# Scores and V·dO of a decode attention backward: eight short matmuls per chunk replaced by two of 512 columns and a selection

## Chip, cores, metric

One core of a Trainium2 chip. The metric is the time of one execution in microseconds (us) of device time; several executions per kernel, medians given.

## The reference

One decode step (one query row, 32 heads, 8192 cached keys of 128 bf16 each), attention plus a gated MLP in parallel, and the gradients of all inputs but B_x. What matters for the time is the K and V cache and their gradients:

```python
q = xn @ wq                      # 32 heads of 128
s = (q . k_cache) * 128**-0.5    # 8192 scores per head
p = softmax(s);  o = p . v_cache # then @ wo
# backward of one head, dO = grad_out @ wo^T:
dp = v_cache . dO                # 8192 values, "V*dO"
u  = p * (dp - sum(p * dp))
dq = u . k_cache;  dK = u x q;  dV = p x dO     # outer products, 2 MB each
```

Per head 4 MB are read (K, V) and 4 MB written (dK, dV).

## The kernel before

A head's K (or V) lies in SBUF as 128 partitions x 64 keys x 128 dimensions. The sums over the dimensions need the dimensions on the partitions, so TensorE transposes. To halve that work, pairs of bf16 are transposed as one fp32 word: `T` makes four 128x128 fp32 transposes (a "chunk", 8 of the 64 keys of every partition) into PSUM, and ScalarE copies them to SBUF. `M` then reads the words as bf16 again; every second value is of one parity.

```python
def T(h, kind, c):
    W3 = kv_tiles[(kind, h)][:].bitcast(F32).rearrange("p (i w) -> p i w", w=P)
    pT = pst()                                  # one of 4 PSUM buffers
    for k in range(4):
        nc.tensor.transpose(pT[:, k * P:(k + 1) * P], W3[:, 4 * c + k, :], ident_f[:])
    KT = kt_tile()
    nc.scalar.copy(KT[:]..., pT[:])

def M(h, kind, c):                              # chunk: stationary; q (or dO) pair: moving
    ...
    for k in range(4):
        i = 4 * c + k
        for par in range(2):
            o = ZW + J * (2 * par + a) - 2 * i  # 64-column window, zero but for columns 2i, 2i+1
            nc.tensor.matmul(S_[kind][:, 0:J], lhsT=KTb[:, k, par, :], rhs=S_["cz"][:, o:o + J],
                             start=(i == 0 and par == 0), stop=(par == 1), ...)
```

The result is one [128, 64] block of scores, keys on the partitions as in the cache. After it come the softmax (`mx`, `mx_bc`, `expo`, `zsum`), the o sum and the dq sum (64 matmuls each, K or V as stationary side), and VectorE's outer products, which overwrite K and V in place; the tile is then stored. Loads and stores go through one FIFO of ten 2 MB slots (`fifo` on SyncE): a load needs a slot whose store is done. TensorE alternates T and M: T(c), M(c-2), T(c+1), M(c-1), and so on, over the 8 K chunks and the 8 V chunks of a head. Before head 2 the MLP runs.

## Time and profile before

| | before |
|---|---|
| time, median | 749.19 us (748.56 to 749.82, 4 runs) |
| bytes moved | 304.63 MB |
| one head, from 255 to 691 us | 21.8 us |
| one head while TensorE had work in stock, 106 to 233 us | 18.1 us |

A head is counted from the first matmul of its o sum to that of the next head's, starts read from the timeline.

The page of the kernel before (span; busy time of TensorE's matmuls and weight loads and of the others; granted clock, DMA share and GB/s in 40 slices; the queue that brings instructions; the chain that ended last, by engine; groups of instructions with busy time, mean ns of one, and idle time before them):

```profile
span 745.6 us, 25013 instructions
...
PE 596.1 (80%) x11263; PEld 568.4 (76%) x11263; DVE 447.8 (60%) x739; ACT 333.4 (45%) x668; POOL 30.4 (4%) x45
...
PEclk9997799999999889999999999998999899988965
DMA  8999999999999999999999999999999999999991
GB/s 327 387 413 421 426 425 425 395 427 426 416 426 427 428 421 428 425 428 425 424 424 429 426 425 417 415 417 424 420 413 425 418 417 419 419 415 418 408 402 72
...
q8 instruction: 88, 1.44, 0.7%
...
DMA 48%; PE 39%; DVE 8%; issue 2%; ACT 1%; SPq 0%; ACTq 0%; DVEq 0%
...
L274 PE MATMUL pT<-ident_f,kv 128*128 128x128 f32 x2048 | 337.1, 289 | 67.4 <-DMA kv<-in_A_k_cache_dram 62.4
...
L293 PEld LDWEIGHTS <-KT 128*128 128x128 bf16 x4096 | 196.8, 100 | 17.7 <-issue 10.6
...
L293 PE MATMUL dA<-cz,KT 128*128 128x64 bf16 x2048 | 107.6, 197 | 8.0 <-ACT qd L310 5.8
```

About half of the chain is DMA, and GB/s stays near 424. The groups mislead in one point: a matmul of L293 is given 197 ns, and there are 4096, so they seem to cost hundreds of us. But these are latencies of pipelined instructions. What one costs is the distance between starts. The timeline of TensorE (start us, us, what) shows it, two transposed chunks (L274) and two M (L293):

```profile
185.77 0.40 PE L293 MATMUL sA<-cz,KT 128*128 128x64 bf16 x8
186.01 0.63 PE L274 MATMUL pT<-ident_f,kv 128*128 128x128 f32 x4
186.48 0.40 PE L293 MATMUL sA<-cz,KT 128*128 128x64 bf16 x8
186.71 0.63 PE L274 MATMUL pT<-ident_f,kv 128*128 128x128 f32 x4
```

From one M to the next M are 186.48 - 185.77 = 0.71 us. Of that the eight matmuls of M take 186.01 - 185.77 = 0.24 us, 30 ns each, weight load included; the four transposes take 0.47.

TensorE's own waits (engine, what waits, for what: us in total, times, longest):

```profile
PE pT L274 <- DMA kv<-in_A_k_cache_dram: 62.4, 22, 5.4
PE hb L358 <- DVE U L365: 14.3, 32, 0.4
```

It waits for K loads, so data come later than TensorE needs them. The waits of the queue that issues loads and stores:

```profile
SPq L101 <- DMA out_dram<-kv: 543.6, 57, 16.9
SPq L101 <- DVE kv L379: 31.9, 11, 7.2
```

A load waits for an earlier store to free its slot: the queue is held by the DMA, not by compute. Windows of 100 us in the middle (us, busy time and count of each engine, granted clock, DMA share, GB/s):

```profile
core 0: us, PE busy (x) PEld busy (x) DVE busy (x) ACT busy (x) POOL busy (x), PEclk, DMA share, GB/s
300.00:400.00 100.00, 80.38 (x1565) 77.11 (x1564) 59.59 (x87) 46.02 (x92) 3.26 (x4) 0.97 1.01 426
400.00:500.00 100.00, 79.86 (x1488) 76.89 (x1485) 56.76 (x93) 45.94 (x93) 3.26 (x4) 0.93 1.01 421
```

### The profile page before, as it was taken

What the parts mean: (1) busy time and instruction counts of PE and PEld (TensorE: products, weight loads), DVE (VectorE), ACT (ScalarE), POOL (GpSimd) and SP (SyncE); (2) the same over time, 40 slices, a digit from 0 to 9 for tenths busy, and PEclk for the clock granted to TensorE, in tenths of its full rate; (3) what the DMA queues carried; (4) which work ended last, traced back from release to release, by engine and by line L of the source; (5) the groups of instructions that cost most, each with busy time, mean ns of one, the idle gap of its engine ahead of it and who ended that gap; (6) DMA issues with size and microseconds to landing.
All of it is one profiled execution on the core that took longest, in us unless ns stands there. A gap on an engine that the chain in (4) does not pass through costs nothing.

```text
span 745.6 us, 25013 instructions
## 1 busy us (share of the span) xinstructions
PE 596.1 (80%) x11263; PEld 568.4 (76%) x11263; DVE 447.8 (60%) x739; ACT 333.4 (45%) x668; POOL 30.4 (4%) x45
## 2 busy tenths in 40 slices
PE   1987698999999779888787897778798788979920
PEld 1886598988998778877686896778798787869820
DVE  4169937677767456656555763646556664656580
ACT  1641055555565355535355553445454353554500
POOL 0100200000000100001000000000000000000000
PEclk9997799999999889999999999998999899988965
DMA  8999999999999999999999999999999999999991
GB/s 327 387 413 421 426 425 425 395 427 426 416 426 427 428 421 428 425 428 425 424 424 429 426 425 417 415 417 424 420 413 425 418 417 419 419 415 418 408 402 72
DMA packets 29136, 304.63 MB, mean 409 GB/s; under 512 B 2836, under 2 KB 5972, under 8 KB 12644
## 3 DMA queue, kind: packets, MB, share of 16 engines
q1 hardware_dynamic: 22736, 276.39, 88.5%
q0 software_dynamic: 5984, 26.30, 8.8%
q8 instruction: 88, 1.44, 0.7%
q10 hardware_dynamic: 308, 0.33, 0.1%
q14 instruction: 20, 0.16, 0.1%
HBM read 151.67 MB, written 151.34 MB: 406 GB/s over the span
## 4 chain that ended last, share of the span: by engine, by line
DMA 48%; PE 39%; DVE 8%; issue 2%; ACT 1%; SPq 0%; ACTq 0%; DVEq 0%
DMA kv<-in_A_k_cache_dram 31%; PE pT L274 17%; DMA out_dram<-kv 13%; PE hb L358 6%; PE hb L373 4%; PE sA L293 4%; DMA kv<-in_A_v_cache_dram 4%; PE dA L293 4%; DVE kv L379 3%; DVE U L365 1%; PE sA L320 1%; PE dh_ps L462 1%; PE hb L363 1%; PE acc L536 1%; PE gu_ps L451 1%
## 5 line engine op out<-in xcount | busy, mean ns | idle before, releaser
L274 PE MATMUL pT<-ident_f,kv 128*128 128x128 f32 x2048 | 337.1, 289 | 67.4 <-DMA kv<-in_A_k_cache_dram 62.4
L276 ACT COPY KT<-pT 128x512 f32<-128x512 f32 x512 | 299.3, 586 | 182.6 <-PE pT L274 149.4
L274 PEld LDWEIGHTS pT<-ident_f,kv 128*128 128x128 f32 x2048 | 224.6, 145 | 71.5 <-issue 69.6
L293 PEld LDWEIGHTS <-KT 128*128 128x128 bf16 x4096 | 196.8, 100 | 17.7 <-issue 10.6
L379 DVE TENSOR_TENSOR kv<-qd,U 128x4096 bf16<-128x4096 bf16 x64 | 146.0, 2284 | 0.0
L379 DVE TENSOR_TENSOR kv<-qd,P 128x4096 bf16<-128x4096 bf16 x64 | 143.4, 2282 | 0.0
L293 PE MATMUL dA<-cz,KT 128*128 128x64 bf16 x2048 | 107.6, 197 | 8.0 <-ACT qd L310 5.8
L293 PE MATMUL sA<-cz,KT 128*128 128x64 bf16 x2048 | 102.7, 192 | 0.4 <-issue 0.3
L358 PEld LDWEIGHTS <-kv 128*128 128x128 bf16 x2048 | 81.7, 106 | 16.5 <-issue 16.5
L358 PE MATMUL hb<-P,kv 128*128 128x64 bf16 x2048 | 82.3, 202 | 14.3 <-DVE U L365 14.3
L375 ACT COPY od_g<-hb 128x2 f32<-128x2 f32 x32 | 5.1, 160 | 160.9 <-PE hb L373 160.9
L373 PE MATMUL hb<-U,kv 128*128 128x64 bf16 x2048 | 70.8, 194 | 5.1 <-issue 5.1
L373 PEld LDWEIGHTS <-kv 128*128 128x128 bf16 x2048 | 66.9, 98 | 6.0 <-issue 5.8
L349 DVE SCALAR_TENSOR_TENSOR U<-dA,P 128x64 bf16<-128x64 f32 x32 | 7.4, 232 | 93.7 <-PE dA L293 93.7
L316 DVE TENSOR_REDUCE mrow<-sA 128x1 f32<-128x64 f32 x32 | 7.2, 224 | 79.5 <-PE sA L293 79.5
L365 DVE SCALAR_TENSOR_TENSOR U<-dA,hb,P 128x128 bf16<-128x128 f32 x32 | 11.4, 355 | 36.3 <-PE hb L363 36.3
L429 DVE SCALAR_TENSOR_TENSOR wq_g<-wq_g,side 128x512 bf16<-128x512 bf16 x40 | 27.3, 683 | 0.0
L340 DVE RECIPROCAL rZ<-sA 128x1 f32<-128x1 f32 x32 | 5.4, 168 | 35.9 <-PE sA L334 35.0
L233 DVE SCALAR_TENSOR_TENSOR side<-wo_g,g_bc 128x640 bf16<-128x640 bf16 x32 | 26.2, 818 | 0.3
L323 DVE TENSOR_REDUCE negM<-sA 128x1 f32<-128x128 f32 x32 | 9.3, 291 | 18.6 <-PE sA L320 18.6
L424 POOL DMA_DIRECT2D out_dram<-wo_g x8 | 6.1, 761 | 295.5 <-DVE cz L298 262.3
L433 POOL DMA_DIRECT2D out_dram<-wq_g x8 | 6.9, 863 | 254.3 <-DVE wq_g L431 254.3
(134 smaller groups left out, 311.5 us busy)
## 6 DMA issues: line engine op xcount, KB each, us to landing
out_dram<-kv SPq DMA_DIRECT2D x64, 2048.0 KB, 31.8
kv<-in_A_k_cache_dram SPq DMA_DIRECT2D x32, 2048.0 KB, 26.9
kv<-in_A_v_cache_dram SPq DMA_DIRECT2D x32, 2048.0 KB, 26.9
out_dram<-wo_g POOLq DMA_DIRECT2D x8, 640.0 KB, 12.1
out_dram<-wq_g POOLq DMA_DIRECT2D x8, 640.0 KB, 13.3
wq_g<-in_A_wq_dram POOLq DMA_DIRECT2D x7, 640.0 KB, 13.8
wo_g<-in_A_wo_dram POOLq DMA_DIRECT2D x7, 640.0 KB, 19.5
kv<-in_B_w_dram SPq DMA_DIRECT2D x2, 1728.0 KB, 16.1
```

Source lines behind the costliest of these rows:

```text
L233: nc.vector.scalar_tensor_tensor(junk[:], G_["wo"][:, hh, :], 1.0, g_bc[:], ALU.mult, ALU.mult, accum_out=G_["do"][:, hh:hh + 1])
L274: nc.tensor.transpose(pT[:, k * P:(k + 1) * P], W3[:, 4 * c + k, :], ident_f[:])
L276: nc.scalar.copy(KT[:].rearrange("p k w -> p (k w)"), pT[:])
L293: nc.tensor.matmul(S_[kind][:, 0:J], lhsT=KTb[:, k, par, :], rhs=S_["cz"][:, o:o + J], start=(i == 0 and par == 0), stop=(par == 1), skip_ ...
L320: nc.tensor.matmul(S_["K"][:, J:J + P], lhsT=S_["mrow"][:].to_broadcast([P, P]), rhs=ident_f[:], start=False, stop=True, skip_group_check= ...
L323: nc.vector.tensor_reduce(S_["negM"][:], S_["K"][:, J:J + P], AX.X, ALU.max, negate=True)
L358: nc.tensor.matmul(S_["hb"][:, 0:RW], lhsT=V3[:, j, :], rhs=S_["P2"][:, j, 0:1].to_broadcast([P, RW]), start=(j == 0), stop=(j == J - 1), ...
L363: nc.tensor.matmul(S_["hb"][:, 2 * RW:2 * RW + 1], lhsT=negones_b, rhs=S_["rdot"][:], start=False, stop=True, skip_group_check=True)
L365: nc.vector.scalar_tensor_tensor(S_["U2"][:], S_["V"][:, 0:J].unsqueeze(2).to_broadcast([P, J, 2]), S_["hb"][:, 2 * RW:2 * RW + 1], S_["P2 ...
L373: nc.tensor.matmul(S_["hb"][:, RW:2 * RW], lhsT=K3[:, j, :], rhs=S_["U2"][:, j, 0:1].to_broadcast([P, RW]), start=False, stop=(j == J - 1) ...
L379: nc.vector.tensor_tensor(dst[:, lo * DH:hi * DH].rearrange("p (j a b) -> p j a b", a=DH // 2, b=2), vec.rearrange("p (a b) -> p a b", b=2 ...
L429: nc.vector.scalar_tensor_tensor(wq_g[:, ci, :], wq_g[:, ci, :], 1.0, dqb, ALU.mult, ALU.mult, accum_out=dxa[:, ci, g:g + 1])
```

## The change

The intent is to swap the two operands of M. The transposed chunk becomes the moving operand, all 512 columns at once, and the q (or dO) pair, zero-padded to 128 columns, becomes the stationary one. Eight weight loads and matmuls per chunk become two. The price: the scores come out turned, 16 useful rows of 512 values, so they are copied to SBUF and turned back by four fp32 matmuls with columns of the identity (`selm`), for K and for V.

```diff
-    ps_t = ctx.enter_context(tc.tile_pool(name="ps_t", bufs=4, space=PSUM))
+    ps_t = ctx.enter_context(tc.tile_pool(name="ps_t", bufs=3, space=PSUM))
+    ps_m = ctx.enter_context(tc.tile_pool(name="ps_m", bufs=1, space=PSUM))
 ...
     def M(h, kind, c):
-        for k in range(4):
-            i = 4 * c + k
-            for par in range(2):
-                o = ZW + J * (2 * par + a) - 2 * i
-                nc.tensor.matmul(S_[kind][:, 0:J], lhsT=KTb[:, k, par, :], rhs=S_["cz"][:, o:o + J], ...)
+        for par in range(2):
+            o = QZ0 + P * (2 * a + par) - 2 * c
+            nc.tensor.matmul(S_[kind][:], lhsT=qz[:, o:o + P], rhs=KTb[:, par, :],
+                             start=(c == 0 and par == 0), stop=(c == NCH - 1 and par == 1))
+
+    def ev(h, kind):
+        XS = kt_tile()
+        nc.scalar.copy(XS[:]..., S_.pop(kind)[:])
+
+    def selm(h, kind):
+        for k in range(4):
+            nc.tensor.matmul(S_["m"][:, b0:b0 + J].rearrange("p (c k t) -> p k c t", k=4, t=2)[:, k, :, :],
+                             lhsT=XS[:, k, :], rhs=ident_f[:, 0:2 * NCH].rearrange("p (c t) -> p c t", t=2), ...)
 ...
     def head(h):            # order: K's eviction and selection ahead of the maximum,
         M(h, "K", NCH - 1)
+        ev(h, "K")
+        T(h, "V", 2)
+        fill_qz(h, 1)
+        selm(h, "K")
         mx(h)
-        T(h, "V", 2)
 ...
+        ev(h, "V")          # V's around half of the o sum; a third chunk of the next head ahead of dq
+        o_sum(h, 0, J // 2)
+        selm(h, "V")
         rdot(h)
-        o_sum(h, 0, J // 2)
+        o_sum(h, J // 2, J)
         dsum(h)
-        o_sum(h, J // 2, J)
+        if pre:
+            T(h + 1, "K", 2)
         dq_sum(h)
```

The rest of the diff moves the small reductions to the new PSUM bank `m` and fills the padded operand `qz` in two steps.

More of the change, by code (lines that the diff above doesn't have):

```diff
@@ L258 @@
     hd = {}
-    ZW = J - 2
-    cz_tiles = []
-    for i in range(2):
-        cz = consts.tile([P, ZW + 4 * J], BF16, name=f"cz{i}")
-        nc.vector.memset(cz[:], 0.0)
-        cz_tiles.append(cz)
     NCH = J // 8
+    QZ0 = 2 * (NCH - 1)
+    qz = consts.tile([P, QZ0 + 4 * P], BF16, name="qz")
+    nc.vector.memset(qz[:], 0.0)
     def new_head(h):
-        hd[h] = dict(kt={}, cz=cz_tiles[h % 2])
+        hd[h] = dict(kt={})
     def T(h, kind, c):
@@ L287, in M, with fill_qz @@
         KTb = S_["kt"].pop((kind, c))[:].rearrange("p k w -> p (k w)").bitcast(BF16).rearrange(
-            "p (k t two) -> p k two t", two=2, t=P)
-        for k in range(4):
-            i = 4 * c + k
-            for par in range(2):
-                o = ZW + J * (2 * par + a) - 2 * i
-                nc.tensor.matmul(S_[kind][:, 0:J], lhsT=KTb[:, k, par, :], rhs=S_["cz"][:, o:o + J],
-                                 start=(i == 0 and par == 0), stop=(par == 1), skip_group_check=True)
-    def fill_cz(h):
+            "p (n two) -> p two n", two=2)
+        for par in range(2):
[3 more added lines that the diff above has]
+    def ev(h, kind):
+        S_ = hd[h]
+        XS = kt_tile()
+        nc.scalar.copy(XS[:].rearrange("p k w -> p (k w)"), S_.pop(kind)[:])
+        S_["xs" + kind] = XS
+    def selm(h, kind):
+        S_ = hd[h]
+        if kind == "K":
+            S_["m"] = ps_m.tile([P, 512], F32, name="m", tag="m")
+        b0 = 0 if kind == "K" else J
+        XS = S_.pop("xs" + kind)
+        for k in range(4):
+            nc.tensor.matmul(S_["m"][:, b0:b0 + J].rearrange("p (c k t) -> p k c t", k=4, t=2)[:, k, :, :],
+                             lhsT=XS[:, k, :], rhs=ident_f[:, 0:2 * NCH].rearrange("p (c t) -> p c t", t=2),
+                             start=(kind == "K" and k == 0), stop=True, skip_group_check=True)
+        S_[kind] = S_["m"][:, b0:b0 + J]
+    def fill_qz(h, a):
         g, hh = divmod(h, GH)
-        nc.vector.tensor_copy(hd[h]["cz"][:, ZW:ZW + 4 * J].rearrange("p (k s) -> p k s", s=J)[:, :, 0:2],
-                              grp[g]["cm"][:, :, :, hh, :].rearrange("p t a m -> p (t a) m"))
+        o = QZ0 + 2 * P * a
+        nc.vector.tensor_copy(qz[:, o:o + 2 * P].rearrange("p (t n) -> p t n", n=P)[:, :, 0:2],
+                              grp[g]["cm"][:, :, a, hh, :])
     def rows_pe(h, ps, first):
@@ L319, in mx_bc @@
         S_ = hd[h]
-        nc.tensor.matmul(S_["K"][:, J:J + P], lhsT=S_["mrow"][:].to_broadcast([P, P]), rhs=ident_f[:],
+        nc.tensor.matmul(S_["m"][:, 2 * J:2 * J + P], lhsT=S_["mrow"][:].to_broadcast([P, P]), rhs=ident_f[:],
                          start=False, stop=True, skip_group_check=True)
         S_["negM"] = small.tile([P, 1], F32, name="negM")
-        nc.vector.tensor_reduce(S_["negM"][:], S_["K"][:, J:J + P], AX.X, ALU.max, negate=True)
+        nc.vector.tensor_reduce(S_["negM"][:], S_["m"][:, 2 * J:2 * J + P], AX.X, ALU.max, negate=True)
     def expo(h):
@@ L333, in zsum @@
         S_ = hd[h]
-        nc.tensor.matmul(S_["K"][:, J + P:J + P + 1], lhsT=ones_b, rhs=S_["rsum"][:],
+        nc.tensor.matmul(S_["m"][:, 2 * J + P:2 * J + P + 1], lhsT=ones_b, rhs=S_["rsum"][:],
                          start=False, stop=True, skip_group_check=True)
@@ L339, in probs @@
         rZ = small.tile([P, 1], F32, name="rZ")
-        nc.vector.reciprocal(rZ[:], S_["K"][:, J + P:J + P + 1])
+        nc.vector.reciprocal(rZ[:], S_["m"][:, 2 * J + P:2 * J + P + 1])
         P2 = small.tile([P, J, 2], BF16, name="P2")
@@ L587, in side_v @@
         elif hh == 3 and g + 1 < NG:
-            prep_cm(g + 1, hd[h]["V"][:, 324:324 + 4 * GH])
+            prep_cm(g + 1, hd[h]["m"][:, 324:324 + 4 * GH])
     def side_pe1(h):
@@ L594, in side_pe1 @@
         elif hh == 3 and g + 1 < NG:
-            prep_q(g + 1, hd[h]["V"][:, 320:320 + GH], False)
+            prep_q(g + 1, hd[h]["m"][:, 320:320 + GH], False)
     def side_pe2(h):
@@ L599, in side_pe2 @@
         if hh == 3 and g + 1 < NG:
-            prep_sel(g + 1, hd[h]["V"][:, 324:324 + 4 * GH])
+            prep_sel(g + 1, hd[h]["m"][:, 324:324 + 4 * GH])
     def outers_a(h):
@@ L617, in head @@
         has_prev = h > 0 and h != MLP_AT
-        had = 2 if h != MLP_AT else 0
+        had = (3 if h else 2) if h != MLP_AT else 0
         if nxt:
@@ L623, in head @@
         side_k(h)
+        if had == 3:
+            M(h, "K", 0)
         for c in range(had, NCH):
@@ L631, in head @@
         M(h, "K", NCH - 1)
+        ev(h, "K")
+        T(h, "V", 2)
+        fill_qz(h, 1)
+        selm(h, "K")
         mx(h)
-        T(h, "V", 2)
+        M(h, "V", 0)
+        T(h, "V", 3)
         mx_bc(h)
         side_m(h)
-        M(h, "V", 0)
-        T(h, "V", 3)
-        expo(h)
         M(h, "V", 1)
         T(h, "V", 4)
+        expo(h)
         M(h, "V", 2)
@@ L655, in head @@
         if nxt:
-            fill_cz(h + 1)
-            rows_pe(h + 1, hd[h]["V"][:, 64:64 + 2 * DH], False)
+            fill_qz(h + 1, 0)
+            rows_pe(h + 1, pst()[:, 0:2 * DH], True)
             rows_act(h + 1)
@@ L678 @@
     prep_cm(0, ps_0[:, 8:8 + 4 * GH])
-    fill_cz(0)
+    fill_qz(0, 0)
     rows_pe(0, ps_0[:, 64:64 + 2 * DH], False)
```

## The prediction

> **What bounds the kernel now.** The DMA: the windows of 25 us show a DMA share near 1.0 and about 424 GB/s from 50 to 700 us. From 255 to 691 us a head takes 21.8 us (start of the o sum to the next head's, timeline). TensorE is close behind: from 106 to 233 us, while it had loaded heads in stock, the waits show almost nothing ahead of it and a head took 18.0 us. Later it waits for K loads (62.4 us in all, view of waits). So TensorE has 3.8 us of slack per head.
>
> **What the change does to TensorE, per head.** It removes 256 weight loads and matmuls of 64 columns. They look costly on the page (197 ns each) but are pipelined: their starts are 28.6 ns apart, so a chunk's eight take 0.23 us, and with four transposes a chunk takes 0.70 us. It adds, per chunk, two matmuls of 512 columns. The MLP stage has 256-column bf16 matmuls 108.5 ns apart, weight loads hidden, as the Trainium skill, "TensorE: Matmul & The Clock Gate", section "Back-to-back issue gap", says (N/2.4 + 2.5). So I estimate 215 ns each: 1024 columns streamed in place of 512. The transposes, 110 ns apart, stay; the long matmul hides their first fp32 weight load (now 0.03 us). Chunk 0.87 us against 0.70, 16 chunks: +2.7 us.
> Selection: 8 fp32 matmuls of two passes; beside a short moving side an fp32 weight load holds the next pass about 110 ns (the sum of the exponentials), so twice 0.85 us: +1.7 us.
> Waits: after the last K chunk the eviction (0.59 us) queues behind another on ScalarE, one transpose covers 0.44 us: +0.5. The third transposed chunk ahead of the dq sum shortens the wait for U, the row broadcast no longer waits: -0.4.
> Sum +4.5 us, range 3.3 to 5.5. ScalarE gets two evictions more (1.2 us) and has room.
>
> **On the critical path.** 18.0 + 4.5 = 22.5 us exceeds the DMA's 21.8, so TensorE becomes the bound of the whole run. Before, without DMA waits, the last head's o sum would start at 106 + 29 x 18.0 = 628 us. After: 628 + 32 x 4.5 = 772 us, plus about 25 us for the last head's outer products, gradients and store (without the store backlog of before).
>
> **Predicted: 797 us, range 770 to 824.** Chances: faster by over 2% 0.02, within 2% 0.05, slower by over 2% 0.93.
>
> **What would show it.** TensorE about 95% busy, clock near 1.0 throughout; waits for K loads below 15 us; DMA share about 0.9 in the middle windows; score matmuls 215 ns apart, a chunk 0.87 us; a head 22 to 23 us in every stretch; a selection group 0.8 to 0.9 us; about 0.5 us of wait ahead of K's selection; the SP queue waiting for VectorE more than now.
>
> **What would make it wrong.** The moving operand takes every second bf16, four bytes apart. All wide bf16 moving operands in the trace are contiguous, and the fp32 ones stream at half rate; if the stride halves the rate, a chunk costs 1.3 us and the time is about 1020 us. If selection or waits are smaller than I think, a head falls below 21.8 us, the DMA stays the bound and only the tail of the last three heads grows: about 755 us. Three PSUM buffers instead of four could add waits on ScalarE.

## The result, and the profile after

| | before | after |
|---|---|---|
| time, median | 749.19 us | 787.09 us (786.77 to 787.32, 4 runs) |
| ratio, 95% interval | | 1.0509 (1.0493 to 1.0525) |
| bytes moved | 304.63 MB | 304.30 MB |
| one head | 21.8 us (18.1 with work in stock) | 22.1 us throughout (120 to 739 us) |
| start of the last head's o sum | 707.5 us | 759.3 us |

A ratio here is the mean time of one kernel's runs over that of the other's of the same rounds, so not quite the ratio of the medians quoted.

The page of the changed kernel, the same parts:

```profile
span 785.5 us, 19851 instructions
...
PE 718.0 (91%) x8625; PEld 575.8 (73%) x8703; DVE 449.3 (57%) x770; ACT 365.2 (46%) x732; POOL 30.4 (4%) x45
...
PEclk9998899999999999999999999999999999999995
DMA  8999999999999999999999999999999999995556
GB/s 326 386 410 422 425 421 388 365 347 420 408 407 423 397 415 405 420 396 422 412 408 420 401 415 402 426 392 418 415 400 427 403 415 410 392 366 249 222 216 280
...
q8 instruction: 68, 1.11, 0.5%
...
PE 82%; ACT 8%; DVE 5%; issue 3%; DMA 2%; SPq 0%; ACTq 0%; DVEq 0%
...
L272 PE MATMUL pT<-ident_f,kv 128*128 128x128 f32 x2048 | 310.0, 274 | 5.0 <-DMA kv<-in_A_k_cache_dram 4.9
L289 PE MATMUL sA<-KT,qz 128*128 128x512 bf16 x480 | 151.2, 390 | 2.2 <-issue 0.2
...
L305 PE MATMUL m<-ident_f,KT 128*128 128x16 f32 x512 | 67.4, 264 | 11.1 <-ACT KT L295 11.1
L305 PEld LDWEIGHTS m<-ident_f,KT 128*128 128x128 f32 x512 | 62.1, 191 | 18.7 <-ACT KT L295 18.7
```

The chain that was half DMA is now TensorE for 82%. TensorE's matmuls fill 91% of the span, and its granted clock reads 1.00 in the windows below (mean of the run 0.979). The timeline of TensorE in one head (L272 transposes, L289 long matmuls, L373 o sum, L305 selection of V):

```profile
293.36 0.60 PE L272 MATMUL pT<-ident_f,kv 128*128 128x128 f32 x4
293.80 0.62 PE L289 MATMUL dA<-KT,qz 128*128 128x512 bf16 x2
294.25 0.60 PE L272 MATMUL pT<-ident_f,kv 128*128 128x128 f32 x4
294.69 0.61 PE L289 MATMUL dA<-KT,qz 128*128 128x512 bf16 x2
...
296.58 0.61 PE L289 MATMUL dA<-KT,qz 128*128 128x512 bf16 x2
297.03 1.14 PE L373 MATMUL hb<-P,kv 128*128 128x64 bf16 x32
298.01 1.04 PE L305 MATMUL m<-ident_f,KT 128*128 128x16 f32 x8
298.90 1.14 PE L373 MATMUL hb<-P,kv 128*128 128x64 bf16 x32
```

From one M to the next are 294.69 - 293.80 = 0.89 us, against 0.71. The two long matmuls take 294.25 - 293.80 = 0.45 us, the four transposes 0.44. The selection of V takes 298.90 - 298.01 = 0.89 us. The timeline gives x8 for its four matmuls: an fp32 one runs as two passes. TensorE's waits:

```profile
PE m L305 <- ACT KT L295: 11.1, 32, 0.6
...
PE pT L272 <- DMA kv<-in_A_k_cache_dram: 4.9, 1, 4.9
```

Only one wait for K loads is left, that of the start. The wait ahead of the selection is 0.35 us per head in K's case, in the view's account; from start to start the gap is 0.60 us where an undisturbed one is 0.11, so 0.49. The waits of the queue for loads and stores:

```profile
SPq L102 <- DVE kv L394: 445.8, 47, 12.0
...
SPq L102 <- DMA out_dram<-kv: 44.7, 5, 17.8
```

Before it waited 543.6 us for stores and 31.9 for VectorE's outer products; now 44.7 and 445.8. The outer products come late, it seems because TensorE's results do: the chain, 82% TensorE, fits that. The windows:

```profile
300.00:400.00 100.00, 96.91 (x1156) 77.73 (x1167) 59.62 (x91) 50.61 (x101) 4.91 (x6) 1.00 1.00 410
400.00:500.00 100.00, 96.96 (x1176) 78.16 (x1186) 57.16 (x98) 50.13 (x102) 3.26 (x4) 1.00 1.00 411
```

The DMA share still reads 1.00, although the DMA is no longer what holds the program; only the GB/s have fallen, from about 424 to 410. The Trainium skill, "Perfetto Trace Analysis", section "Identifying the Most-Contended Engine", says that the occupancy of the 16 DMA engines misleads and that the utilization of the memory's bandwidth should be used. This trace agrees.

### The profile page after: what moved, and what is told of

Its sections match the earlier page's. It is cut to its first block, busy times and chain, and to the rows that moved or that the text cites. A ratio compares the mean times of both kernels' runs of the same rounds, so it can differ in the third digit from the quotient of the medians.

```text
span 785.5 us, 19851 instructions
## 1 busy us (share of the span) xinstructions
PE 718.0 (91%) x8625; PEld 575.8 (73%) x8703; DVE 449.3 (57%) x770; ACT 365.2 (46%) x732; POOL 30.4 (4%) x45
## 2 busy tenths in 40 slices
DMA packets 29117, 304.30 MB, mean 387 GB/s; under 512 B 2837, under 2 KB 5973, under 8 KB 12645
## 4 chain that ended last, share of the span: by engine, by line
PE 82%; ACT 8%; DVE 5%; issue 3%; DMA 2%; SPq 0%; ACTq 0%; DVEq 0%
PE pT L272 26%; PE sA L289 13%; PE dA L289 13%; PE hb L373 8%; PE m L305 8%; PE hb L388 8%; ACT KT L274 4%; ACT KT L295 2%; DVE kv L394 2%; DMA kv<-in_A_k_cache_dram 2%; PE m L349 2%; ACT E L344 1%; PE m L335 1%; PE hb L378 1%; PE dh_ps L477 1%
## 5 line engine op out<-in xcount | busy, mean ns | idle before, releaser
L272 PEld LDWEIGHTS pT<-ident_f,kv 128*128 128x128 f32 x2048 | 253.5, 142 | 101.5 <-issue 5.5
L272 PE MATMUL pT<-ident_f,kv 128*128 128x128 f32 x2048 | 310.0, 274 | 5.0 <-DMA kv<-in_A_k_cache_dram 4.9
L289 PE MATMUL sA<-KT,qz 128*128 128x512 bf16 x480 | 151.2, 390 | 2.2 <-issue 0.2
L289 PE MATMUL dA<-KT,qz 128*128 128x512 bf16 x466 | 146.6, 388 | 3.3
L289 PEld LDWEIGHTS <-qz 128*128 128x128 bf16 x1024 | 97.8, 102 | 5.8 <-issue 0.2
L373 PEld LDWEIGHTS <-kv 128*128 128x128 bf16 x2048 | 71.5, 98 | 8.3
L305 PE MATMUL m<-ident_f,KT 128*128 128x16 f32 x512 | 67.4, 264 | 11.1 <-ACT KT L295 11.1
L305 PEld LDWEIGHTS m<-ident_f,KT 128*128 128x128 f32 x512 | 62.1, 191 | 18.7 <-ACT KT L295 18.7
L373 PE MATMUL hb<-P,kv 128*128 128x64 bf16 x2048 | 72.9, 192 | 0.0
L388 PEld LDWEIGHTS <-kv 128*128 128x128 bf16 x2048 | 67.0, 97 | 4.8 <-issue 1.0
L380 DVE SCALAR_TENSOR_TENSOR U<-m,hb,P 128x128 bf16<-128x128 f32 x32 | 11.4, 355 | 30.4 <-PE hb L378 30.4
L234 DVE SCALAR_TENSOR_TENSOR side<-wo_g,g_bc 128x640 bf16<-128x640 bf16 x32 | 26.2, 817 | 0.3
## 6 DMA issues: line engine op xcount, KB each, us to landing
wo_g<-in_A_wo_dram POOLq DMA_DIRECT2D x7, 640.0 KB, 19.9
```

The costliest lines, as they stand in the source:

```text
L234: nc.vector.scalar_tensor_tensor(junk[:], G_["wo"][:, hh, :], 1.0, g_bc[:], ALU.mult, ALU.mult, accum_out=G_["do"][:, hh:hh + 1])
L289: nc.tensor.matmul(S_[kind][:], lhsT=qz[:, o:o + P], rhs=KTb[:, par, :], start=(c == 0 and par == 0), stop=(c == NCH - 1 and par == 1))
L305: nc.tensor.matmul(S_["m"][:, b0:b0 + J].rearrange("p (c k t) -> p k c t", k=4, t=2)[:, k, :, :], lhsT=XS[:, k, :], rhs=ident_f[:, 0:2 * N ...
L373: nc.tensor.matmul(S_["hb"][:, 0:RW], lhsT=V3[:, j, :], rhs=S_["P2"][:, j, 0:1].to_broadcast([P, RW]), start=(j == 0), stop=(j == J - 1), ...
L380: nc.vector.scalar_tensor_tensor(S_["U2"][:], S_["V"][:, 0:J].unsqueeze(2).to_broadcast([P, J, 2]), S_["hb"][:, 2 * RW:2 * RW + 1], S_["P2 ...
L388: nc.tensor.matmul(S_["hb"][:, RW:2 * RW], lhsT=K3[:, j, :], rhs=S_["U2"][:, j, 0:1].to_broadcast([P, RW]), start=False, stop=(j == J - 1) ...
```

## The experiments

### Which half of the change is it: a two-by-two

The four corners are: short or long matmuls, without or with eviction and selection. All three new kernels keep the order, PSUM buffers and look-ahead of the changed kernel.

**short_nosel** (correct): the old M in the new order.

```diff
-            nc.tensor.matmul(S_[kind][:], lhsT=qz[:, o:o + P], rhs=KTb[:, par, :], ...)
+            nc.tensor.matmul(S_[kind][:, 0:J], lhsT=KTb[:, k, par, :], rhs=S_["cz"][:, o:o + J], ...)
-        ev(h, "K") ... selm(h, "K") ... ev(h, "V") ... selm(h, "V")
```

> The changed kernel's order, PSUM buffers and look-ahead, but with the eight short matmuls per chunk of before and no selection (result correct). Theory (TensorE work per head is the bound, order is harmless): TensorE needs about 17.6 us per head, less than the DMA's 21.8, so the time falls back to 744 to 754 us. Rival (the new order, three PSUM buffers for transposes instead of four, or the third chunk ahead cost the time by disturbing transfers): it stays above 770 us.

Measured: 748.36 us (747.89 to 748.76), ratio to before 1.0001 (0.9986 to 1.0016). Neither the order nor the third PSUM buffer costs anything that the time shows.

**short_sel** (wrong result): short_nosel with eviction and selection put back.

```diff
+        ev(h, "K")   # copies S[:, 0:64] eight times over: 512 values, as many as in the change
+        selm(h, "K")
```

> As short_nosel, with the eviction and the fp32 selection matmuls of the change put back (their data are not the scores, result wrong on purpose). Theory: selection and its waits add 2 to 2.8 us of TensorE per head, about 20.2 us, still under the DMA's 21.8: 747 to 760 us, only the tail grows. Rival (the serial step eviction, selection, maximum is what lengthens a head, whatever TensorE has to do): 775 us or more.

Measured: 748.96 us (748.57 to 749.49), ratio 1.0010 (0.9995 to 1.0025). While TensorE had work in stock (115 to 433 us) a head took 19.9 us instead of 18.1, and still the time is that of before.

**long_nosel** (wrong result): the change without eviction and selection.

```diff
-        ev(h, "K") ... selm(h, "K") ... ev(h, "V") ... selm(h, "V")
```

> The change without eviction and selection (the rows are not turned back, result wrong on purpose). Theory: about 22.05 - 2.5 = 19.5 us of TensorE per head, under the DMA's 21.8: 747 to 760 us, so each half of the change alone hides in the slack and only both together show. Rival (the long matmuls alone are the loss): 775 us or more.

Measured: 740.85 us (740.77 to 743.20), ratio 0.9911 (0.9895 to 0.9928). A head took 19.9 us (113 to 431 us). The time is under the range I had given: this kernel is even 1% faster than before, a point to which best_split returns. TensorE's waits for K loads in long_nosel, against 62.4 us before:

```profile
PE pT L272 <- DMA kv<-in_A_k_cache_dram: 14.9, 8, 4.7
```

TensorE's head in the four corners is thus 18.1 us (short_nosel, 106 to 233 us), 19.9, 19.9 and 22.1. Each half of the change lengthens it by 1.8 us, and each alone costs no time, because it stays within the slack that TensorE has under the DMA. Both together, 4.0 us, exceed it. The cost appears only in the sum. The rivals (the order, and either half alone) fall.

How large is that slack? Not 21.8 - 18.1 = 3.7 us: then heads of 22.1 us would cost 32 x 0.3 = 10 us, and 38 were measured. The 21.8 us are the DMA's pace after 255 us, when the stock is used up. Of the 29 heads from 106.1 to 707.5 us the first seven took 18.1, and all 29 took 20.7 on average. So my estimate from these starts is that a TensorE which needs over about 20.7 us for every head comes late at the end, and that the slack over the run is 20.7 - 18.1 = 2.6 us. Runs that come below agree: pack_best with 20.8 us a head takes 745.32 us, about the time of the kernel before, and sel_later and long_contig with 21.7 and 21.8, not above 21.8, take 773.04 and 776.38. In the spans of the kernels before and after the loss adds up so: the third head begins 120.2 - 106.1 = 14.1 us later, 29 heads take 22.0 in place of 20.7 us, or 37.7 us more, and from the start of the last o sum to the end it is 26.2 in place of 38.1 us, 11.9 less. The sum is 39.9 us, the difference of the spans (785.5 - 745.6).

### What bounds each kernel: fewer bytes

**before_half** and **after_half** (wrong results): half of each head's dV is not stored.

```diff
-        fifo((dkc if kind == "K" else dvc)[h], t[:])
+        n = KVN // 2 if kind == "V" else KVN
+        fifo((dkc if kind == "K" else dvc)[h][:, 0:n], t[:, 0:n])
```

> The kernel before, but only half of each head's V gradient is stored (1 MB less per head, result wrong on purpose). Theory (bound by the DMA): a head has 8.0 MB in place of 9.05, 18.9 us at 424 GB/s, close to TensorE's 18.0: 655 to 690 us. If TensorE bounded it, it would not change.

> The changed kernel, with the same half of V's gradient not stored (result wrong on purpose). Theory (bound by TensorE although the DMA share reads 1.0 in most windows): a head stays at 22.0 us, the time at 775 to 788 us, while the DMA share falls. Rival (the DMA, slower through the new order of loads and stores, is the bound): the time falls by 60 us or more, as the kernel before does.

Measured: before_half 667.86 us (667.08 to 668.40), ratio 0.8924; after_half 787.81 us (787.59 to 789.61), which is 1.0533 of the kernel before and the time of the changed kernel, as if no byte had been saved. The windows of before_half:

```profile
300.00:400.00 100.00, 91.73 (x1890) 88.58 (x1888) 72.94 (x111) 54.33 (x110) 4.13 (x5) 1.00 1.01 423
400.00:500.00 100.00, 90.14 (x1796) 86.37 (x1794) 67.46 (x102) 55.31 (x111) 4.92 (x6) 1.00 1.01 416
```

and of after_half:

```profile
300.00:400.00 100.00, 97.27 (x1167) 77.41 (x1163) 59.42 (x90) 50.61 (x101) 3.26 (x4) 1.00 0.95 362
400.00:500.00 100.00, 97.71 (x1187) 78.04 (x1187) 57.06 (x97) 50.14 (x102) 3.26 (x4) 1.00 0.95 368
```

before_half still moves about 420 GB/s and finishes its heads faster; after_half moves 362 to 368 GB/s and TensorE is at 97 to 98 of 100 us. This is the plainest proof: the kernel before is bound by the DMA, the changed one by TensorE. (In before_half a head takes 18.1 us from 105 to 449 us, TensorE's own pace with work in stock, so there both are at their limit.) Note the DMA share of 0.95 in after_half: a DMA that moves 14% less than the 424 GB/s of before looks nearly full.

### The size of the terms

**long_contig** (wrong result): the moving operand reads 512 neighbouring bf16.

```diff
-            "p (n two) -> p two n", two=2)
+            "p (two n) -> p two n", two=2)
```

> The change with the moving operand read as 512 neighbouring bf16 in place of every second one (result wrong on purpose). The measured pitch of the long matmuls is 227 ns where I had estimated 215. If the four-byte step is the reason, the pitch falls to 215 ns, a head loses 32 x 0.012 = 0.4 us and the time falls to 772 to 780 us. If the step is free, pitch 227 ns and 785 to 789 us.

Measured: 776.38 us (776.20 to 777.40), ratio 1.0379 (1.0363 to 1.0394). The starts of neighbouring long matmuls fell from 227 to 216 ns, a head from 22.1 to 21.8 us. So the step of four bytes costs 5% of a long matmul. The estimate of 215 ns in the prediction was right for a contiguous operand only.

**sel_bf16** (correct): rows evicted as bf16 and selected by bf16 matmuls.

```diff
-        XS = kt_tile()                                    # fp32
+        XS = t_tile()[:, 0:4 * P].rearrange(...)          # bf16
-                             lhsT=XS[:, k, :], rhs=ident_f[:, 0:2 * NCH]...
+                             lhsT=XS[:, k, :], rhs=ident_bf[:, 0:2 * NCH]...
```

> The change with the rows evicted as bf16 and turned back by bf16 selection matmuls (one pass each, meant to be correct within tolerance). Theory: an fp32 pass held TensorE 112 ns because of its weight load, 16 passes per head; bf16 ones should start about 30 ns apart, 8 per head, so a head loses about 1.5 us, 22.05 to 20.5, under the DMA's 21.8: 740 to 754 us. Rival (the serial step eviction and selection costs the time, not the fp32 passes): 778 us or more.

Measured: 742.99 us (742.82 to 743.13), ratio 0.9929 (0.9914 to 0.9944). The selection's matmuls in sel_bf16:

```profile
L305 PE MATMUL m<-ident_bf,KT 128*128 128x16 bf16 x256 | 16.1, 171 | 11.1 <-ACT KT L295 11.1
```

256 in place of 512, one pass each, and most of their starts are 25 to 26 ns apart (a few 39) where the fp32 passes are 112. A head takes 20.5 us (116 to 690 us). The wait of 11.1 us ahead of K's selection is still there, so the gain is the fp32 passes and not the serial step.

**sel_later** (correct): K's selection one chunk later, fp32 kept.

```diff
+        M(h, "V", 0)
+        T(h, "V", 3)
         selm(h, "K")
         mx(h)
-        M(h, "V", 0)
-        T(h, "V", 3)
+        M(h, "V", 1)
         mx_bc(h)
```

> The change with K's selection one chunk later, behind one more long-matmul pair and four transposes, so that the eviction is done when it comes; fp32 kept. Theory: with TensorE as the bound its 0.49 us gap ahead of K's selection is paid 32 times and goes away: a head 21.5 to 21.7 us, 769 to 778 us. Rival (the gap overlaps with something else that bounds): 785 us or more.

Measured: 773.04 us (772.81 to 773.28), ratio 1.0330 (1.0313 to 1.0348), so 14 us under the changed kernel for a gap of 0.49 us x 32 = 15.7. The wait for the eviction is gone from TensorE's waits. While TensorE is the bound, every 0.1 us of a head is 3.2 us of time.

### A version that beats both

**best** (correct): sel_bf16 and sel_later together.

> bf16 selection and K's selection one chunk later, both together (meant correct). Theory: a head 20.0 to 20.1 us of TensorE, under the DMA's 21.8, so no more gain than sel_bf16 has: 739 to 746 us, and about 1% under the kernel before. If the steadier TensorE pace is what sped sel_bf16 up, it is no faster than sel_bf16; if TensorE still bounded sel_bf16, it is 8 us or more faster.

Measured: 741.83 us (741.78 to 741.85), ratio 0.9918 (0.9904 to 0.9931): 0.8% under the kernel before, clear of the noise but small. A head needs 20.2 us of TensorE (113 to 517 us), and the small step from sel_bf16 (1.2 us) says that TensorE no longer bounds.

**pack** (correct): 32-column stationary windows; the two long matmuls write different 32-row groups of PSUM.

```diff
-            nc.tensor.matmul(S_[kind][:], lhsT=qz[:, o:o + P], rhs=KTb[:, par, :], ...)
+            nc.tensor.matmul(S_[kind][32 * par:32 * par + 32, :], lhsT=qz[:, o:o + 32], rhs=KTb[:, par, :], ...)
-                             lhsT=XS[:, k, :], rhs=ident_f[...
+                             lhsT=XS[0:64, k, :], rhs=sel2[0:64, ...   # adds the two groups
```

> The change with 32-column stationary windows: the two long matmuls of a chunk write PSUM partitions 0 to 31 and 32 to 63, and a 64-row fp32 selection adds them (meant correct). If the two run at the same time in different column groups of the array, as the Trainium skill, 'TensorE: Matmul & The Clock Gate', section 'Part 3: Packing small matmuls - row/col tiling', describes, their starts fall from 227 ns to a few ns apart, a head to about 18.5 us, DMA-bound: 740 to 755 us. If they run one after the other, or changing between full and column-tiled use costs about as much as it saves, 780 us or more.

Measured: 803.09 us (802.29 to 803.78), ratio 1.0736 (1.0722 to 1.0751). Timeline of TensorE in pack (L275 transposes, L292 long matmuls):

```profile
400.86 0.40 PE L292 MATMUL sA<-KT,qz 128*32 128x512 bf16 x2
401.19 0.66 PE L275 MATMUL pT<-ident_f,kv 128*128 128x128 f32 x4
401.78 0.40 PE L292 MATMUL sA<-KT,qz 128*32 128x512 bf16 x2
```

The two long matmuls do run at the same time: their starts are 3 to 4 ns apart, and both together last 0.40 us, as each record does. But from M to M are 401.78 - 400.86 = 0.92 us, more than the 0.89 of the changed kernel. The time went into longer starts where the mode changes: the last transpose holds the next long matmul for 0.20 us instead of 0.11, the long ones hold the first transpose for 0.33 instead of 0.23, and the first transpose holds the second for 0.17 instead of 0.11 (starts of the trace's single records). The Trainium skill, "TensorEngine Tiling (Array Packing)", section "Key Properties", says that changing the tiling mode drains the engine. The longer starts fit that. They add up to about 0.25 us for a change to column tiles and back, more than the 0.22 us that packing saves here. Whether the drain is all of it, or the packed pair also streams more slowly, no run separates.

**pack_best** (correct): pack with best's selection.

> pack, best's bf16 selection and best's later K selection together (meant correct). If packing works: TensorE about 17 us per head, DMA-bound with more waits for K loads than best, 738 to 750 us, no gain over best, since TensorE's time no longer counts. If packing does not work, the same as best, 739 to 748 us.

Measured: 745.32 us (744.64 to 747.31), ratio 0.9963 (0.9950 to 0.9977). A head takes 20.8 us, not the 17 that I expected, without a wait for K loads after the start; no gain over best.

**best_split** (correct): best with every long matmul cut into four.

```diff
-            nc.tensor.matmul(S_[kind][:], lhsT=qz[:, o:o + P], rhs=KTb[:, par, :], ...)
+            for q in range(4):
+                nc.tensor.matmul(S_[kind][:, q * P:(q + 1) * P], lhsT=qz[:, o:o + P],
+                                 rhs=KTb[:, par, q * P:(q + 1) * P], ...)
```

> best with each 512-column matmul cut into four of 128 columns: the same columns streamed, the same operands, but eight weight loads and matmuls per chunk as the kernel before has (meant correct). It asks why best and long_nosel are about 1% faster than the kernel before, while short_sel, which has TensorE pace like theirs but short matmuls, is not. If the number of TensorE instructions is the reason (their fetch shares the DMA engines: 0.7% against 0.5% of them), the time goes back to 746 to 750 us. If the reason is the other operand (transposed chunks as stationary side) or something else, it stays at 740 to 744 us. The starts should be about 57 ns apart and a head at most 20.6 us, under the DMA's 21.8.

Measured: 749.45 us (749.24 to 749.94), ratio 1.0017 (1.0003 to 1.0031). Starts 58 ns apart, a head 20.4 us (114 to 359 us): TensorE has nearly the pace of best, but the gain over the kernel before is gone. So the gain of 1% comes with the smaller number of TensorE instructions (matmuls and weight loads together). The granted clock is not the reason: it is 0.97 in both (mean). The queue that brings instructions (q8) in best (packets, MB, share of the 16 engines):

```profile
q8 instruction: 66, 1.08, 0.6%
```

and in best_split:

```profile
q8 instruction: 90, 1.47, 0.8%
```

From 500 to 680 us best moves 422 GB/s and best_split 416. The fetch of instructions goes through the same DMA engines, and it grew by 0.39 MB and 0.2% of their span. That alone is 1.5 us of the 7.6. What makes up the rest is not settled: fetches may disturb the large transfers more than their share says, or the extra weight loads may. No run separates these.

## Why the prediction was right

Predicted 797 us, range 770 to 824; measured 787.09. The steps, one by one:

- **Bound before: the DMA, with 3.8 us of TensorE slack per head.** The bound is right: before_half falls by 80 us. The two paces are right too, 18.1 against 21.8 us, but as slack of the whole run 3.8 us is too much; counted with the early heads it is about 2.6 (see the two-by-two). The predicted time does not hang on it, because it adds up TensorE's heads.
- **The short matmuls cost 28.6 ns, not 197.** Right. This is the reading that decided the sign. Mean duration times count would give 4096 x 0.195 = 799 us before and 1024 x 0.39 = 399 us after, a large saving that does not exist.
- **A chunk 0.87 us against 0.70.** Measured 0.89 against 0.71. The long matmul was sized at 215 ns and is 227; long_contig shows that the four-byte step is the difference. 16 chunks cost about +2.9 us, predicted +2.7. The fear that the step halves the rate (1020 us) was unfounded.
- **Selection +1.7 us.** Measured 2 x 0.89 = 1.8. The reason given, fp32 weight loads that hold the next pass about 110 ns, is the measured 112 ns; sel_bf16 removes the cost.
- **Waits +0.5 and -0.4.** The gap ahead of K's selection is 0.49 us, and sel_later gets 14 us back for it. The second term was mis-sized: the head grew by 22.1 - 18.1 = 4.0 us, where chunks, selection and this gap give 2.9 + 1.8 + 0.5 = 5.2. So about 1.2 us of other waits went away, not 0.4. The view of TensorE's waits accounts for them. Two of its lines for the kernel before, in the seven heads from 106 to 233 us:

```profile
PE hb L358 <- DVE U L365: 3.1, 7, 0.4
PE dA L293 <- ACT qd L310: 2.9, 5, 1.0
```

  With the others there it shows 8.8 us, 1.26 per head. For the changed kernel, in the 28 heads from 120 to 739 us, it shows 1.8 us beside the 9.4 ahead of K's selection, 0.06 per head. The wait for U, which the prediction named, and that of M for the copy of the row broadcast (`qd`) are 0.9 of the 1.26. But the new order alone does not gain the 1.2 us: in short_nosel (106 to 233 us) these two are gone, others make 8.4 us, and the head is still 18.1 us. In long_nosel (113 to 431 us, 16 heads) 1.4 us are left. So it is the longer M that fills the waits: by its starts it adds 2.9 us to a head, and between these two runs the head grew by 1.8.
- **The sum, 797 us.** The last o sum was predicted at 772 us and began at 759.3, because 29 heads took 22.0 us instead of 22.5. From there to the end of the span it took 26.2 us instead of 25. Per head, chunks and selection came out 0.3 us larger than predicted and the removed waits 0.8 larger: the errors offset in part, which is luck, and the rest is most of the overestimate of 10 us.
- **TensorE becomes the bound of the whole run.** Right: after_half does not change the time, the chain is 82% TensorE, and the wait for K loads fell to 4.9 us (predicted below 15).
- **"A head falls below 21.8 us, the DMA stays the bound", about 755 us.** Wrong, as an alternative that did not occur in the changed kernel: sel_later's head is 21.7 us, and it takes 773.04.
- **DMA share about 0.9 in the middle.** Wrong: it read 1.00, at 410 GB/s. The share does not fall in proportion when the DMA is given less to do. The predicted mechanism stands on the GB/s and on after_half, not on the share. TensorE busy was predicted at about 95% and is 91% over the span, 97% in the middle windows.

## What to carry to other kernels

The cost of a pipelined matmul is the distance from its start to the next start. Here this was 25 to 29 ns for bf16 matmuls of 16 and of 64 columns alike, 216 to 227 for 512 columns, and 112 for an fp32 pass of 16 columns; before swapping operands, count the columns that each form streams. When one engine has slack under another, price a change per unit of work against that slack, and take the slack over the whole run, stock at the start included: two additions that each cost nothing can cost 5% together. Work added to an engine that has short waits fills them first. To see what bounds a program, take bytes or work away in an experiment and look whether the time follows; a busy share of 1.00 proves little.

## What the Trainium skill lacked or had wrong

- "TensorE: Matmul & The Clock Gate", section "Back-to-back issue gap": N/2.4 + 2.5 holds here for a contiguous bf16 moving operand (216 ns at 512 columns, run long_contig). The section has no figure for a step: every second bf16 gave 227 ns. The same section's sustained 131 ns per matmul at 512 columns is not reached by the full-width matmuls of any run here.
- The same page, section "Part 4: PE-mode transpose", gives about 275 ns for a 128x128 bf16 transpose in one kernel's context. The records of fp32 transposes in the changed kernel last 274 ns, but start 109 ns apart, at a granted clock of 1.00; the pitch is what counts.
- "TensorEngine Tiling (Array Packing)", section "Key Properties", names the drain at a change of mode without a price. In pack the starts around a change to column-tiled matmuls and back were about 0.25 us longer.
- "Perfetto Trace Analysis", section "Identifying the Most-Contended Engine", takes the weight-load busy share, beside the share of the peak in arithmetic (not worked out here), as a measure for TensorE. Here it was 76% when the DMA was the bound and 73% when TensorE was; matmul busy (80% and 91%) went the right way, as the change put work from weight loads into streamed columns.
- "Runtime: NRT & Kernel Launch", section "Instruction fetch mechanics", has no figure for what the fetch takes from a program that the DMA engines bound. Here 0.39 MB more of it (1.47 against 1.08 MB, with 25,586 against 19,442 instructions) came with 7.6 us more time.
